# Normed attention and a gated MLP on one Trainium2 core: transfers that wait for their planned time, and a planner with stepwise inputs

## The chip, the core and the metric

The program runs on one core of a Trainium2 chip. The metric is device time in microseconds. Before the change nine runs gave a median of 286.65 us (283.63 to 288.15).

A core has five engines, each with its own instruction queue that it works off strictly in order: TensorE (PE; its weight loads are listed as PEld), VectorE (DVE), ScalarE (ACT), GpSimd (POOL) and SyncE (SP), which here only issues DMA transfers. Engines wait for each other, and for transfers, by semaphores. SBUF is the on-chip memory, PSUM the accumulators that PE writes. A transfer issued by SP or ACT goes through a hardware queue (q1 for SP), one issued by POOL through a software queue (q0).

## What is computed

Eight batches of twelve heads, 448 positions, head size 64. q and k are normed by their root mean square, the scores go through a softmax, and the result, heads side by side (768 columns), goes through a gated MLP with a spatial product.

```python
q_n, k_n = rmsnorm(q, g_q), rmsnorm(k, g_k)        # over the last axis
attn = softmax(q_n @ k_n.T / sqrt(64)) @ v         # per head
x = attn.transpose(0, 2, 1, 3).reshape(8, 448, 768)
h = np.maximum(x @ w_in, 0.0)                      # 768 -> 1024
u, v = h[..., :512], h[..., 512:]
v_n = (v - mean(v)) / sqrt(var(v) + 1e-6)
v_s = einsum('ts,bsd->btd', w_spatial, v_n) + b_spatial[None, :, None]
out = (u * v_s) @ w_out                            # 512 -> 768
```
Inputs and output are float32; the matrix products run in bfloat16.

## The kernel before

**Tiling.** Attention runs over 24 groups G, three per batch, four heads each. For a group, q and k are loaded as 128x896 (`load`, L306), squared (L407 on ACT, L409 on DVE or POOL), summed per row of 64 (`reduce`, L417, always DVE), turned into 1/rms by a logarithm and an exponential on ACT (`rstd`, L423, L424), and scaled to bfloat16 (L431, DVE or POOL). The first six groups are transposed by PE against an identity (`turn`, L448) and copied from PSUM by DVE (`turned`, L457 for q, L459 for k, which also multiplies by the product of g_q and g_k, `g2_col`); the later ones by a DMA transpose (L466). Seven rounds of scores follow (L493, 4 matmuls each, into two PSUM buffers `pss`), each with one exp on ACT over 128x896 (L516). `sums` (L534, 16 matmuls) adds up the exps, `recip` (L541, L542) inverts the sums on ACT, `values` (L552, 2 x 16 matmuls) multiplies by v, and DVE writes the product with the reciprocal into `xt` (L559).

**The MLP** of a batch begins when its six `xt` pieces stand: `unit_v` (L591 for 128 rows, L595 for the last 64), relu on ACT or DVE (L567, L569), row statistics (L615, L616), `ln_rstd` (L622, L623) and `ln_apply` (L630); `unit_u` (L642); `unit_s` (L658), the product with the transposed `w_spatial` (`w_spT`, made by PE, L381); the gate on DVE (L663); `unit_o` (L682, L703), its copy out of PSUM on ACT (L670) or DVE (L672), and the store (L694, L714). Stores go out on SP's queue; in the last batch every second one on ACT's.

**The order** is written by a planner at build time. Every piece of work is a `Task` with a cost (occupancy, latency) on each engine that may do it, a position `pos` in time (smaller is more urgent), tasks that it depends on, PSUM and SBUF buffers that it takes (`get`) or uses, a tile mode on PE (a change of mode costs), and for transfers an earliest time `after` and a length `dma`. The planner goes through simulated time. For each engine it takes the tasks that could start within `LOOK` of the earliest one, and of these the one with the smallest `pos`; the engine whose choice starts first emits its task. Each engine's queue so gets a fixed order. The times of the plan are not in the program: `after` sets a transfer's place in its queue, and a transfer starts when its queue comes to it and its buffer is free.

```python
LOOK = {"PE": 0.15, "ACT": 0.1, "DVE": 0.1, "POOL": 0.2, "SP": 0.2}
...
if t.dma:
    dma = max(dma, at + occ + 1.6) + t.dma
    t.done = dma + 1.3
```
`due(G)` (L291) is the position of a group: 6.3 us apart for the first three, 9.8 for the others. The loads of the first three groups have `after` 0, the others due(G) - 26. There are five raw buffers each for q and k. v of a batch is loaded by four transfers on POOL's queue (L344), w_in by two (L356), w_sp and w_out by one each (L362, L367). [...]

`dummies` (L284) are matmuls on the identity with no use but to keep PE running; `fill` puts them into PE's planned gaps of more than 0.6 us up to 25.5 us. The g rows are loaded by SP (L312, L313), multiplied by DVE (L319), turned into a column by a PE matmul (L326) and copied out of PSUM by DVE (L330).

Of the kernel before, what the change touches and what calls it, by code (L numbers as in the profile page):

```python
# [44 lines left out]
class Task:  # L45
    def __init__(self, name, costs, pos, emit, deps=(), get=(), use=(), mode=None, dma=0.0, after=0.0,
                 port=False):
        self.name, self.costs, self.pos, self.emit = name, costs, pos, emit
        self.deps = [d for d in deps if d is not None]
        self.get = list(get)  # L50
        self.held = list(use)
        self.use = self.get + self.held
        for b in self.use:
            b.left += 1
        self.mode = mode
        self.dma = dma
        self.after = after
        self.port = port
        self.done = None


class Planner:
# [4 lines left out]
    LOOK = {"PE": 0.15, "ACT": 0.1, "DVE": 0.1, "POOL": 0.2, "SP": 0.2}  # L67

    def __init__(self, tc, trace=None):
        self.tc = tc  # L70
        self.tasks = []
        self.trace = trace
        self.port_user = None
# [13 lines left out]
    def add(self, *a, **k):  # L87
        t = Task(*a, **k)
        self.tasks.append(t)
        return t  # L90

    def start_of(self, t, e, free):
        at = max(free[e], t.after)
        if e == "POOL" or (e == "DVE" and t.port):
            at = max(at, self.locked)
        for d in t.deps:
            if d.done is None:
                return None
            at = max(at, d.done)
        if any(b.slot is None for b in t.held):  # L100
            return None
        need = {}
        for b in t.get:
            if b.pool.ordered and b.seq != b.pool.taken + need.get(b.pool, 0):
                return None
            need[b.pool] = need.get(b.pool, 0) + 1
        for p, n in need.items():
            f = sorted(p.free)
            if f[n - 1] == math.inf:
                return None  # L110
            at = max(at, f[n - 1])
        return at

    def run(self, fill=None):
        free = {"PE": 0.0, "ACT": 0.0, "DVE": 0.0, "POOL": 0.0, "SP": 0.0}
        mode, dma = None, 0.0
        self.locked = 0.0
        left = list(self.tasks)
        while left:
            ready = {}  # L120
            for t in left:
                for e in t.costs:
                    at = self.start_of(t, e, free)
                    if at is not None:
                        ready.setdefault(e, []).append((at, t))
            best = None
            for e, c in ready.items():
                end = {}
                first = min(at for at, _ in c)
                for at, t in c:  # L130
                    if at > first + self.LOOK[e]:
                        continue
                    if len(t.costs) > 1:
                        mine = at + t.costs[e][1]
                        other = min(
                            (self.start_of(t, o, free) + t.costs[o][1] for o in t.costs if o != e))
                        if other < mine - 1e-6:
                            continue
                    s = t.pos
                    if e == "PE" and t.mode != mode:  # L140
                        s += 0.6
                    key = (s, at)
                    if best_e_is(end, key):
                        end["k"], end["t"], end["at"] = key, t, at
                if "t" in end and (best is None or end["at"] < best[0]):
                    best = (end["at"], e, end["t"])
            at, e, t = best
            occ, lat = t.costs[e]
            if e == "PE" and t.mode != mode:
                sw = 0.095  # L150
                occ, lat = occ + sw, lat + sw
                mode = t.mode
            if e == "PE" and fill is not None:
                fill(free["PE"], at)
            for b in t.get:
# [3 lines left out]
                p.taken += 1  # L159
            t.emit(e)  # L160
            self.hand_over(t, e)
            free[e] = at + occ
            t.done = at + lat
            if (e == "POOL" and t.dma == 0) or (e == "DVE" and t.port):
                self.locked = at + occ
            if t.dma:
                dma = max(dma, at + occ + 1.6) + t.dma
                t.done = dma + 1.3
# [5 lines left out]
            if self.trace is not None:  # L174
                self.trace.append((at, at + occ, t.done, e, t.name))
            left.remove(t)


def best_e_is(end, key):
    return "k" not in end or key < end["k"]  # L180
# [11 lines left out]
def kernel(  # L192
# [61 lines left out]
    plan = Planner(tc, TRACE)  # L254
# [15 lines left out]
    ident = const.tile([128, 128], BF, name="ident")  # L270
    make_identity(nc, ident)
# [14 lines left out]
    def fill(a, b):  # L286
        if b < 25.5 and b - a > 0.6:
            dummies(int((b - max(a, 2.0) - 0.4) / 0.11))


    def due(G, r=0.0):  # L291
        x = G + r / 7.0
        return 12.0 + (6.3 * x if x < 3 else 18.9 + 9.8 * (x - 3))
# [6 lines left out]
    for G in range(NGT):  # L300
        b, g = divmod(G, NG)
        for i in range(2):
            bf = raw[G, i] = Buf(P_raw[i])

            def emit(e, bf=bf, src=(q_x, k_x)[i][b][g]):
                sync.dma_start(out=bf.t, in_=src)  # L306

            raw_t[G, i] = add(f"load{i} G{G}", {"SP": (0.6, 0)}, due(G) - 26 + i * 0.1, emit, get=[bf], dma=1.4,
                              after=0.0 if G < 3 else due(G) - 26)

    def emit(e):
        sync.dma_start(out=g_row[:, 0], in_=bass.AP(tensor=g_q.tensor, offset=g_q.offset, ap=[[0, 1], [0, 2], [1, D]]))  # L312
# [438 lines left out]
```

## Time and profile before

| | us |
|---|---|
| median of 9 runs | 286.65 |
| lowest, highest | 283.63, 288.15 |
| the profiled execution | 283.63 |
| its span, first to last instruction | 281.9 |
| PE busy | 267.2 |
| ACT busy | 229.0 |
| DVE busy | 195.1 |
| POOL busy | 146.7 |

The mean granted PE clock was 0.997. The 24 loads each of q and k (448 KB) took 5.2 and 6.2 us from issue to landing in the median, the two of w_in (768 KB each) 21.5, w_out 16.1, w_sp 15.6.

In the views below each row gives a start and a length in microseconds, or a busy time. "x16" counts instructions, `out<-in` names tiles without their buffer numbers, and what stands in square brackets is the idle time of the engine before the row and what ended it. In a table of stretches each engine's busy time is followed by its instructions, then come the granted clock (1.00 is full), the share of the DMA engines and GB/s. In a chain of waits each row is the work that released the next.

### The profile page before, as it was taken

Reading aid. Unit: us, or ns where it says so; the run is one execution under the profiler, and the core shown is the slowest. Engines: PE = TensorE matmul, PEld = TensorE weight load, DVE = VectorE, ACT = ScalarE, POOL = GpSimd, SP = SyncE. Lnnn points to the kernel's source line nnn. Section 1 sums busy time; section 2 is a strip of 40 time slices with the busy share of each in tenths; the row PEclk is TensorE's granted clock in tenths of the full one; section 3 lists DMA queues with packets and bytes.
Section 4 is the critical chain, followed back from the end, with each engine's and each line's share of the span. In section 5 each row is a group of like instructions: output and inputs, shape, how many; then the busy total and the mean of one; then the engine's idle time right before and its main releaser. Section 6 shows DMA issues by size and latency. Waiting matters only on the chain.

```text
span 281.9 us, 7090 instructions
## 1 busy us (share of the span) xinstructions
PE 267.2 (95%) x2875; PEld 124.8 (44%) x2875; DVE 195.1 (69%) x332; ACT 229.0 (81%) x369; POOL 146.7 (52%) x122
## 2 busy tenths in 40 slices
PE   7877899999999999999999999999999999999992
PEld 7733464444444444444444444444344443444450
DVE  3986999987777668878885678776775468343630
ACT  4798899978987888878887988879899878676522
POOL 8131546177595776896888497498885000000000
PEclk9999999999999999999999999999999999999998
DMA  7999999477999899995999589998992460007006
GB/s 246 322 294 244 274 282 161 49 195 123 214 221 199 195 177 242 229 242 119 255 240 224 155 205 223 171 305 189 175 216 50 98 165 2 0 12 189 1 5 191
DMA packets 65450, 50.01 MB, mean 177 GB/s; under 512 B 41929, under 2 KB 61898, under 8 KB 65418
## 3 DMA queue, kind: packets, MB, share of 16 engines
q1 hardware_dynamic: 51274, 40.61, 59.6%
q0 software_dynamic: 13824, 8.27, 20.8%
q10 hardware_dynamic: 320, 0.69, 0.7%
q8 instruction: 22, 0.36, 0.5%
q14 instruction: 10, 0.08, 0.1%
HBM read 38.55 MB, written 11.01 MB: 176 GB/s over the span
## 4 chain that ended last, share of the span: by engine, by line
PE 71%; DMA 11%; ACT 6%; DVE 4%; POOL 3%; issue 3%; ACTq 1%; SPq 0%; POOLq 0%; DVEq 0%
PE ps L642 12%; PE pss L493 11%; PE ps L552 11%; PE ps L591 10%; PE ps L658 8%; PE ps L682 8%; PE ps L534 6%; DMA vt<-in_v_dram 5%; ACT et L516 3%; DMA kr<-nk 3%; DMA qf<-in_q_dram 2%; PE ps L595 2%; ACT osb L670 1%; PE ps L703 1%; DVE ms L417 1%
## 5 line engine op out<-in xcount | busy, mean ns | idle before, releaser
L516 ACT ACTIVATE et<-pss 128x896 bf16<-128x896 f32 x168 | 144.0, 916 | 13.4 <-PE pss L493 13.0
L417 DVE TENSOR_REDUCE ms<-sq 128x14 f32<-128x896 f32 x48 | 51.5, 1074 | 8.1 <-ACT sq L407 4.2
L493 PE MATMUL pss<-qT,kT 64*64 64x448 bf16 x672 | 50.3, 362 | 5.7 <-ACT et L516 3.8
L431 POOL TENSOR_TENSOR nq<-qf,rs 128x896 bf16<-128x896 f32 x19 | 32.1, 1688 | 39.5 <-ACT rs L424 32.8
L559 DVE TENSOR_TENSOR xt<-ps,rc 128x448 bf16<-128x448 f32 x48 | 29.4, 623 | 17.6 <-PE ps L552 11.3
L552 PE MATMUL ps<-et,vt 128*32 128x448 bf16 x768 | 41.1, 354 | 0.5 <-DMA vt<-in_v_dram 0.5
L642 PE MATMUL ps<-xt,w_in 128*128 128x448 bf16 x192 | 40.3, 354 | 0.0
L409 POOL TENSOR_TENSOR sq<-kf 128x896 f32<-128x896 f32 x18 | 30.2, 1680 | 14.1 <-DVE nk L431 8.0
L431 POOL TENSOR_TENSOR nk<-kf,rs 128x896 bf16<-128x896 f32 x19 | 32.1, 1688 | 10.1 <-PE ps L448 7.3
L682 PE MATMUL ps<-w_out,gt 128*128 128x384 bf16 x192 | 34.8, 327 | 0.6 <-DVE gt L663 0.6
L591 PE MATMUL ps<-w_in,xt 128*128 128x512 bf16 x144 | 33.7, 380 | 0.0
L663 DVE TENSOR_TENSOR gt<-ps,us 128x448 bf16<-128x448 f32 x32 | 19.9, 623 | 15.6 <-PE ps L658 13.2
L409 POOL TENSOR_TENSOR sq<-qf 128x896 f32<-128x896 f32 x16 | 27.0, 1685 | 6.2 <-DVE kT L474 2.4
L493 PEld LDWEIGHTS <-kT 64*64 64x64 bf16 x672 | 14.3, 104 | 35.9 <-issue 32.3
L658 PE MATMUL ps<-w_spT,vn 128*128 128x448 bf16 (+1 forms) x128 | 27.7, 354 | 0.0
L552 PEld LDWEIGHTS <-vt 128*32 128x32 bf16 x768 | 18.7, 96 | 19.8 <-issue 7.8
L642 PEld LDWEIGHTS <-w_in 128*128 128x128 bf16 x192 | 17.0, 98 | 21.2 <-issue 7.6
L672 DVE COPY osb<-ps 128x384 f32<-128x384 f32 x28 | 15.5, 556 | 14.3 <-PE ps L682 8.9
L615 DVE BATCH_NORM_STATS2 s<-vs 128x6 f32<-128x512 bf16 (+1 forms) x32 | 22.0, 687 | 4.5 <-ACT vs L567 4.1
L682 PEld LDWEIGHTS <-gt 128*128 128x128 bf16 x192 | 17.1, 98 | 17.5 <-issue 6.2
L534 PE MATMUL ps<-et,ones 128*32 128x448 bf16 x384 | 22.8, 355 | 0.1
L344 POOL DMA_DIRECT2D vt<-in_v_dram x32 | 21.6, 692 | 0.0
(65 smaller groups left out, 265.6 us busy)
## 6 DMA issues: line engine op xcount, KB each, us to landing
qf<-in_q_dram SPq DMA_DIRECT2D x24, 448.0 KB, 5.2
kf<-in_k_dram SPq DMA_DIRECT2D x24, 448.0 KB, 6.2
out_dram<-osb SPq DMA_DIRECT2D x45, 192.0 KB, 2.9
vt<-in_v_dram POOLq DMA_DIRECT2D x16, 192.0 KB, 7.5
vt<-in_v_dram POOLq DMA_DIRECT2D x16, 144.0 KB, 8.3
w_in<-in_moe_w_in_dram POOLq DMA_DIRECT2D x2, 768.0 KB, 21.5
out_dram<-osb SPq DMA_DIRECT2D x15, 96.0 KB, 3.7
w_out<-in_moe_w_out_dram POOLq DMA_DIRECT2D x1, 768.0 KB, 16.1
```

What stands on the lines that cost most here:

```text
L409: eng_of[e].tensor_tensor(out=sqb.t, in0=r.t, in1=r.t, op=ALU.mult)
L417: dve.tensor_reduce(out=ms.t[:, i], in_=sqb.t.rearrange("p a (s d) -> p (a s) d", d=D), axis=AX.X, op=ALU.add)
L431: eng_of[e].tensor_tensor(out=nb.t.rearrange("p s a d -> p a s d"), in0=r.t.rearrange("p a (s d) -> p a s d", d=D), in1=P_rs[G % 4][:, i]. ...
L493: pe.matmul(out=ps[64 * h:64 * h + 64, a, 0:S], lhsT=kb[64 * a:64 * a + 64, slot, 64 * xk:64 * xk + 64], rhs=qb[64 * a:64 * a + 64, :, 64 ...
L516: act.activation(out=eb.t[:, r], in_=bf.t[:, :, 0:S], func=AF.Exp, bias=0.0, scale=1.0)
L534: pe.matmul(out=bf.t[32 * l:32 * l + 32, 0:S], lhsT=ones[:, (0 if c < 3 else 1 + x), :], rhs=eb.t[:, r, a, :], start=(c == 0), stop=(c == ...
L552: pe.matmul(out=bf.t[32 * l:32 * l + 32, 0:S], lhsT=vb.t[:, 2 * (g + 3 * a) + x, c, half::2], rhs=eb.t[:, r, a, :], start=(c == 0), stop=( ...
L559: dve.tensor_tensor(out=xb.t[:, j * S:j * S + S], in0=bf.t[:, 0:S], in1=rc.t, op=ALU.mult)
L591: pe.matmul(out=bf.t, lhsT=xb.t[:, j * S + 128 * c:j * S + 128 * c + 128], rhs=w_in[:, j, DH:DF], start=(j == 0), stop=(j == 5))
L642: pe.matmul(out=bf.t[:, 0:S], lhsT=w_in[:, j, 128 * f:128 * f + 128], rhs=xb.t[:, j * S:j * S + S], start=(j == 0), stop=(j == 5))
L658: pe.matmul(out=bf.t[:, 0:S], lhsT=vn.t[0:kp, c, 128 * f:128 * f + 128], rhs=w_spT[0:kp, c, :], start=(c == 0), stop=(c == 3))
L682: pe.matmul(out=bf.t[:, 0:384], lhsT=gt.t[:, f, 128 * c:128 * c + 128], rhs=w_out[:, f, 384 * h:384 * h + 384], start=(f == 0), stop=(f == 3))
```

## The change

1. **Transfers.** A transfer with `after` above 0 gets a semaphore wait (`hold_back`) for the ACT or DVE instruction that ended last in the plan before the transfer's planned start. Its planned length changes (w_in 4.8 to 4.0, w_sp 3.0 to 2.2, w_out 5.0 to 4.5, stores 1.4 to 1.6, the tail of a transfer 1.3 to 0.9), and `after` of several.
2. **Planner.** A dependence can be a pair (task, early): the task may start `early` before the other is done, as its later steps alone need it. `LOOK` is larger, waiting costs `WAIT` per microsecond in the choice, and an engine can have a `bias` against a task.
3. **Parts.** Group 0's squares and reduces are halved (ACT alone squares there), its scaling, transposes and copies are cut in 4 and 3 of 7. `sums` and `values` of groups 0 to 2 are cut in 3 + 1 rounds, `unit_v0` and `unit_v1` of batch 0 in 4 + 2 steps.
4. **Queues.** The g rows are loaded from POOL's queue, ahead of the identity. In the last batch every second store goes on POOL's queue, not ACT's.
5. `fill` takes gaps from 0.4 us.

```diff
+def stepwise(deps, step):
+    return [(d, step * i) for i, d in enumerate(deps)]
...
-    LOOK = {"PE": 0.15, "ACT": 0.1, "DVE": 0.1, "POOL": 0.2, "SP": 0.2}
+    LOOK = {"PE": 0.3, "ACT": 0.9, "DVE": 1.1, "POOL": 0.6, "SP": 0.2}
+    WAIT = 4.0
+    SWITCH = 0.095
+    KEEP = 0.6
...
+    def hold_back(self, t, at, first):
+        ended = [x for x in self.recent if x[0] <= at + 0.2]
+        if t.dma and t.after > 0 and ended:
+            self.tc.add_manual_dep(
+                first, max(ended, key=lambda x: x[0])[1].name,
+                mybir.DependencyInfo(mybir.DependencyClass.Sync, mybir.DependencyReason.DATA),
+                reason="transfer")
...
-                    s = t.pos
+                    s = t.pos + self.WAIT * (at - first)
...
-                t.done = dma + 1.3
+                t.done = dma + 0.9
...
+    for i, g in enumerate((g_q, g_k)):
+        pool.dma_start(out=g_row[:, i], in_=bass.AP(tensor=g.tensor, offset=g.offset, ap=[[0, 1], [0, 2], [1, D]]))
     make_identity(nc, ident)
...
-        if b < 25.5 and b - a > 0.6:
-            dummies(int((b - max(a, 2.0) - 0.4) / 0.11))
+        if b < 25.5 and b - a > 0.4:
+            dummies(int((b - max(a, 2.0) - 0.25) / 0.11))
...
-        return 12.0 + (6.3 * x if x < 3 else 18.9 + 9.8 * (x - 3))
+        return 11.0 + (6.6 * x if x < 3 else 19.8 + 9.6 * (x - 3))
...
-                              after=0.0 if G < 3 else due(G) - 26)
+                               after=0.0 if G < 3 else (9.0, 20.0, 27.0)[G - 3] if G < 6 else due(G) - 26)]
...
-    g_t = add("g2", {"DVE": (0.3, 0.3)}, due(0) - 2.5, emit, deps=[g_t])
+    g_t = add("g2", {"DVE": (0.3, 0.3)}, -90.0, emit, after=6.2)
...
-                                 use=[bf] if parts else [], dma=1.4, after=9.0 if b == 0 else due(3 * b) + (2 if b == 1 else -8)))
+                                 use=[bf] if parts else [], dma=1.4, after=4.0 if b == 0 else 33.0 if b == 1 else due(3 * b) - 8))
...
-        w_t.append(add("w_in", {"POOL": (0.9, 0)}, 5.0, emit, dma=4.8, after=13.0))
+        w_t.append(add("w_in", {"POOL": (0.9, 0)}, 0.0, emit, dma=4.0, after=10.0 + 4.0 * a))
...
-    wsp_load = add("w_sp", {"POOL": (1.0, 0)}, 29.0, emit, dma=3.0, after=18.0)
+    wsp_load = add("w_sp", {"POOL": (1.0, 0)}, 29.0, emit, dma=2.2, after=24.0)
...
-    wout_t = add("w_out", {"POOL": (1.0, 0)}, 36.0, emit, dma=5.0, after=34.0)
+    wout_t = add("w_out", {"POOL": (1.0, 0)}, 36.0, emit, dma=4.5, after=36.0)
...
+        halves = [slice(0, 1), slice(1, 2)] if G == 0 else [slice(0, 2)]
...
+                if G == 0:
+                    costs = {"ACT": costs["ACT"]}
...
+                        bias={"ACT": 0.5 if G == 1 else 5.0} if G else None,
...
+            pieces = [(0, 4), (4, NS)] if G == 0 else [(0, NS)]
...
+        cuts = [(0, 3), (3, 4)] if G < NG else [(0, 4)]
+        need = [[(exps[G, r], 0.19 * max(0, (r % 3 if r < 6 else 3) - c0)) for r in range(6 if c1 < 4 else 7)]
+                for c0, c1 in cuts]
...
+            for j0, j1 in [(0, 4), (4, 6)] if b == 0 and c < 2 else [(0, 6)]:
...
-            a = add(f"unit_s{f} b{b}", {"PE": (0.757, 1.02)}, pos, emit, deps=vns + wspT_t, get=[bf], use=[vn], mode="G")
+            a = add(f"unit_s{f} b{b}", {"PE": (0.757, 1.02)}, pos, emit, deps=stepwise(vns, 0.19) + wspT_t, get=[bf], use=[vn], mode="G")
...
-                    (act if y and b == B - 1 else sync).dma_start(out=o[2 * c + y], in_=ob.t[64 * y:64 * y + 64, :])
-            add(f"store{c} b{b}", {"SP": (0.9 if b < B - 1 else 0.5, 0)}, pos + 1, emit, deps=cs, use=[ob], dma=1.4)
+                    (pool if y and b == B - 1 else sync).dma_start(out=o[2 * c + y], in_=ob.t[64 * y:64 * y + 64, :])
+            add(f"store{c} b{b}", {"SP": (1.2, 0) if b < B - 1 else (0.6, 0)}, pos + 1, emit, deps=cs, use=[ob], dma=1.6)
```

## The prediction

> **What bounds the kernel now.** I read the page first, then the busy time by stretches, the chain of waits of the first 40 us, the timelines of its start and end, and the rows of one tile.
>
> ```profile
> PE 267.2 (95%) x2875; PEld 124.8 (44%) x2875; DVE 195.1 (69%) x332; ACT 229.0 (81%) x369; POOL 146.7 (52%) x122
> DMA  7999999477999899995999589998992460007006
> ```
> TensorE (PE) is the bound on average, and the DMA engines are full for the first 35 us. By stretches (columns: PE, PEld, DVE, ACT, POOL, clock, DMA, GB/s):
>
> ```profile
> 10.00:15.00 5.00, 3.29 (x47) 2.49 (x44) 4.98 (x6) 3.54 (x7) 0.00 (x0) 1.00 1.20 303
> 20.00:25.00 5.00, 4.22 (x70) 2.00 (x67) 2.11 (x4) 4.45 (x9) 0.00 (x0) 1.00 1.06 246
> 50.00:60.00 10.00, 10.00 (x120) 4.53 (x112) 9.91 (x17) 9.12 (x14) 4.66 (x3) 1.00 0.48 76
> 36.45:260.00 223.55, 222.10 (x2414) 96.79 (x2414) 159.45 (x276) 191.49 (x311) 130.65 (x94) 1.00 0.84 172
> ```
> From 36.45 to 260 us PE is idle for 223.55 - 222.10 = 1.45 us in all. Its matmuls are the same in both programs (only 5 dummies fewer), so beyond these 1.45 us a new order can win only by fewer changes of tile mode, in the start and in the tail. The chain of waits of the start:
>
> ```profile
> 4.39 2.04 POOL vt L344 x3
> 6.42 15.48 DMA vt<-in_v_dram
> 22.04 1.71 PE ps L552 x31
> 23.77 0.06 DVE xt L559
> ```
> The first v load lands at 21.90, and PE, whose queue is in order, stops before `values` of group 0. The timeline shows what else was late:
>
> ```profile
> 7.44 0.14 DVE L330 COPY g_col<-ps 128x1 f32<-128x1 f32 x1
> ...
> 13.21 0.57 PE L493 MATMUL pss<-qT,kT 64*64 64x448 bf16 x8 [1.05 <-DVE kT L459]
> ...
> 13.93 7.37 ACT L516 ACTIVATE et<-pss 128x896 bf16<-128x896 f32 x9
> ...
> 23.09 1.31 DVE L559 TENSOR_TENSOR xt<-ps,rc 128x448 bf16<-128x448 f32 x2 [2.83 <-PE ps L552]
> ```
> VectorE (DVE) sat 2.83 us behind the v load. ScalarE (ACT) sets the pace by 21 exps (0.82 us each: nine in 7.37) for groups 0 to 2; the last ended at 35.9.
>
> **The first scores (group 0 in parts, g rows on GpSimd).** GpSimd (POOL) now issues two g loads before it builds the identity. Their issue is not in the trace: by the other POOL issues it lies at 0.58 (w_sp) to 0.82 (w_out), and below that at 0.37 (SP's bias load). I take 0.6, since they are the smallest. The identity, ready at 1.37, comes 1.2 us later (0.7 to 1.6). 38 dummies wait for it and run 0.11 each (43 in 4.77), until 6.8. Behind them stands the g2 matmul; its copy on DVE started 0.87 after it (6.57 to 7.44), so now at 7.7. DVE's new order puts this copy ahead of three of the four half reduces, which therefore all wait for it. A whole reduce costs 1.07 at a pitch of 1.0; a half lies between 0.5 and 0.65, and I take 0.54: the last ends at 9.45, against 7.51 before. Ln and exp follow 0.77 later as before (10.2; before 8.28). During them DVE squares k of group 1 (1.0). Then come four scaled pieces (2.15, from 10.45) and four turned pieces (0.33, 0.26, 0.38, 0.30): kT is complete at 13.9, before 13.16. What the split pipelines, the g2 wait takes. First exp 14.4, before 13.93.
>
> **Squares leave ACT.** ACT squared eleven times at 0.95, now once and in four halves; DVE does three squares more, POOL five. ACT's own time is not the limit there, DVE's queue is. After kT of group 0 DVE holds two reduces, a square, a reduce, two scaled, qT, a reduce and kT before group 1 can be scored: 2.0 + 1.0 + 1.0 + 2.0 + 0.56 + 1.0 + 0.62 = 8.2, so 22.1; before, kT of group 1 ended at 18.28. ACT's order has rstd of group 2 ahead of group 1's exps, and it needs the reduce that ends at 21.5; with rstd (0.6) and the reciprocal (1.15) the first exp of group 1 starts at 23.4 and the seventh ends at 29.2 (before 27.9). Group 2 adds 7 x 0.82, a reciprocal, an rstd (0.58) and some 0.4 of waits: 37.1, against 35.9. **1.2 us later.**
>
> **Transfers wait.** q and k of group 3, w_in, w_sp, the later v and w_out now wait for an ACT or DVE instruction. Only six q/k loads (2.7 MB) and v (0.67 MB) run at first: at the 303 GB/s of the row at 10 to 15 us that is 11 us from 2 us, so v lands near 13 and is not needed before 21. This removes PE's 0.45 and DVE's 2.83; the 1.2 above has that in it. What is queued behind a held load: on SP other loads, transposes and stores, on POOL squares and scalings. The holds name the plan's neighbour in time, and five raw buffers lie between a load and its use, so I take 0, with 0 to +2 as bounds (a late transpose already cost 9.37 us of the chain at 142 us, and PE only 0.2 there).
>
> [...]
>
> ```profile
> L344 POOL DMA_DIRECT2D vt<-in_v_dram x32: 662/687/823, 4.3 to 202.3; - x32
> ...
> DMA to landing us min/median/max: 3.5/7.9/15.5
> ```
> [...] The sum goes by the row, 0.
>
> **PE fills its waits (stepwise inputs).** Two pieces of unit_v (8 matmuls, 1.73) and the sums in parts go ahead of the last exps; in exchange w_sp's transposes (2.0) come later. The comparison is made where batch 0's v units go on. Before, that is 40.87. The new order has by then done 12 score matmuls (0.75) and those 8 more, so level is 40.87 + 0.75 + 1.73 = 43.4. Following ACT on (two exps, reciprocal, two exps from 37.7: the buffers of the third score block come free at 42.2) PE gets there at 42.2 + 0.5 + 2.0 = 44.7, or 43.4 if ACT does not hold it. I take **+1.0** for the start, with bounds -2 (the g2 wait not binding: kT of group 1 then 1.5 earlier, and the waits of 0.5) and +3.
>
> **Steady state.** Mode changes on PE after group 2's scores: 200 become 192. One costs 0.10 to 0.11 (unit_s of 4 matmuls takes 0.76 after a wide unit, 0.86 to 0.87 after values): **-0.85**. Nine relu, five vs and some k scalings pass from ACT to DVE, some 11 us over 200, beside PE. The 1.45 us of idle time I keep; bounds -1.45 and +2.
>
> **Tail.** The second stores go from ACT's queue to POOL's.
>
> ```profile
> 275.55 0.84 PE L703 MATMUL ps<-w_out,gt 128*64 128x384 bf16 x8
> ...
> 277.35 0.49 ACT L670 ACTIVATE osb<-ps 128x384 f32<-128x384 f32 x1 [0.65 <-ACT osb L670]
> ...
> 277.87 0.50 ACTq L714 DMA_DIRECT2D out_dram<-osb  x1
> ```
> PE ended at 276.39, the last copy started at 277.35, because ACT had issued three stores (0.5 each). Now it can start at 276.55: -0.8. POOL's issue is longer by 0.2, and its landing lies between ACT's 3.0 and 3.5 (the shortest v load): **-0.3**, bounds -0.8 and +0.5.
>
> The sum, on the profiled execution (283.63: span 281.9 and 1.7 around it): 283.63 + 1.0 - 0.85 - 0.3 = 283.5. But this was the fastest of nine; the median is 3.0 above it. The trace does not show what the slower ones lose. A v load that lands later moves everything behind it, which the change would end; if it is something else, the 3.0 stay. I take a little under half: **284.8**.
>
> **Rivals.**
> *The spread goes and the start gains* (0.26): with v at 13 nothing of 0.45 and 2.83 is left and the copy of g2 is not late: 283.5 less 2 to 3 from the start, 281 to 283 as a median. For it: v heads the chain. Against: DVE's order.
> *DVE becomes the bound, slower* (0.26): DVE is at 9.91 of 10 in 50 to 60 us already. The new order gives it 2.5 us more work before batch 0's last xt; where a DVE square or scaling meets a POOL one it doubles (2.14 instead of 1.08 at 27.66), three times being 3.2. If PE waits for these, 283.63 + 2.5 + 3.2 = 289.3, and up to 292 with the spread. It decides where kT of group 1 is later than 23.5 or PE is idle over 3 us between 36 and 62.
> *The holds do nothing* (0.08): the named instructions were done long before, v still lands at 20 or later: 286.65 - 0.85 - 0.3 = 285.5.
>
> **How the numbers follow.** My case has 0.40, with its own range from 282.5 to 287.5. About 1% is what a measurement tells from no change: below 283.8 is faster, above 289.5 slower. Faster: the first rival and a quarter of my case, 0.36. Slower: 0.26. Within: 0.38. The range that leaves out 2 in 10 goes from 281 to 291.
>
> **What would show it.** Right: v landed before 16; the g2 copy after 7.3; first exp at 14 to 15; kT of group 1 at 21.5 to 23; PE idle under 2 us from 44 to 260; osb of the last rows within 0.3 of PE's end. Wrong: a first exp before 13; PE waiting for a DMA in mid run; runs spread over 3 us as before.

## The result, and the profile after

The changed kernel takes 287.94 us (median of 17 runs, 287.17 to 289.43; an eighteenth, at 285.98, is on record beside them), the kernel before 286.52 (54 runs, 282.99 to 289.03): a ratio of 1.0091, 95% interval 1.0065 to 1.0116. It is about 0.9% slower; the forecast was 284.8, 0.65% faster. Medians here are over all runs of a kernel; ratios leave disturbed runs out.

| profiled execution | before | after |
|---|---|---|
| time | 283.63 | 287.95 |
| span | 281.9 | 286.2 |
| PE's last matmul ends | 276.39 | 279.19 |
| from there to the span's end | 5.51 | 7.01 |
| mean granted clock | 0.997 | 0.985 |

So 2.80 of the 4.3 us lie ahead of PE's end and 1.50 behind it. The page of the changed kernel has, against the rows shown of before, 15 us more on DVE, 12 us less on ACT and the same PE time. One slice in 40 has a much lower clock (the lower last slice is there before, too):

```profile
PE 267.8 (94%) x2870; PEld 125.2 (44%) x2870; DVE 209.7 (73%) x357; ACT 217.5 (76%) x348; POOL 157.2 (55%) x132
...
PEclk9999995999999999999999999999999999999998
```

The start of the changed kernel in its timeline. The copy of g2 ends at 8.07 and the reduces stand behind it; the first scores go at 13.83, the first exp at 14.57, and the exps of group 1 at 23.25:

```profile
7.91 0.16 DVE L361 COPY g_col<-ps 128x1 f32<-128x1 f32 x1 [0.78 <-PE ps L357]
...
13.83 0.89 PE L550 MATMUL pss<-qT,kT 64*64 64x448 bf16 x8 [0.31 <-DVE kT L512]
...
14.57 2.54 ACT L573 ACTIVATE et<-pss 128x896 bf16<-128x896 f32 x3 [4.32 <-PE pss L550]
...
23.25 6.64 ACT L573 ACTIVATE et<-pss 128x896 bf16<-128x896 f32 x8
```

The busy time by stretches answers the row 36.45 to 260 of before (columns: PE, PEld, DVE, ACT, POOL, clock, DMA, GB/s). After:

```profile
42.10:48.95 6.85, 6.85 (x71) 4.69 (x67) 5.15 (x10) 2.48 (x4) 3.93 (x3) 0.50 1.02 248
60.00:80.00 20.00, 18.84 (x211) 8.76 (x208) 18.55 (x25) 16.73 (x28) 13.19 (x8) 1.00 0.77 186
80.00:260.00 180.00, 179.77 (x1940) 78.10 (x1939) 135.10 (x237) 149.48 (x234) 109.86 (x79) 1.00 0.86 175
```

Before, in the same stretches:

```profile
42.10:48.95 6.85, 6.85 (x54) 3.23 (x54) 6.35 (x12) 6.79 (x12) 4.32 (x5) 1.00 1.03 161
60.00:80.00 20.00, 20.00 (x224) 8.63 (x222) 15.31 (x26) 18.22 (x31) 14.02 (x10) 1.00 0.84 206
80.00:260.00 180.00, 178.55 (x1920) 76.38 (x1913) 121.21 (x212) 151.06 (x244) 105.57 (x76) 1.00 0.83 171
```

Two things are to be seen. After 49 us the two are level in PE's idle time: the new order has 1.16 us between 60 and 80 and 0.23 later, where before had 1.45. And between 42.10 and 48.95 PE is busy all the time, at a granted clock of 0.50. What stands ahead of that stretch, on PE and on DVE:

```profile
39.46 0.94 PE L618 MATMUL ps<-et,vt 128*32 128x448 bf16 x16
41.47 0.60 PE L412 MATMUL ps<-ident,w_sp 64*64 64x64 bf16 x9 [1.07 <-DVE xt L627]
...
43.00 2.28 PE L412 MATMUL ps<-ident,w_sp 64*64 64x64 bf16 x35
45.21 1.04 PE L660 MATMUL ps<-w_in,xt 128*128 128x512 bf16 x2
```

```profile
37.79 0.97 DVE L422 CAST w_spT<-bst 1x448 bf16<-1x448 f32 x1
38.79 1.09 DVE L449 TENSOR_TENSOR sq<-qf 128x896 f32<-128x896 f32 x1
39.80 1.08 DVE L449 TENSOR_TENSOR sq<-kf 128x896 f32<-128x896 f32 x1
40.80 0.62 DVE L627 TENSOR_TENSOR xt<-ps,rc 128x448 bf16<-128x448 f32 x1
```

PE has written the values of group 2 and needs a PSUM buffer that only DVE's `xt` can free; two of the four are held by the begun pieces of `unit_v`. DVE has a row copy of the bias and two squares ahead of that `xt`, so PE stands still for 1.07 us. Then come 35 narrow transposes of w_sp in a row. The end of the chain of waits is now on POOL:

```profile
279.24 0.52 POOL out_dram L765
279.76 0.23 issue
279.99 0.55 POOLq L818
```

Its last row, at 279.99, is at the time of POOL's last store; the span ends at 286.2, 5.6 us after that row's end. What fills these 5.6 us stands among the instructions of the program's last line (L818, before L746). Each row gives the shortest, the median and the longest of its instructions in ns, then the first and the last start. After, and then before:

```profile
L818 POOLq DRAIN  x3: 46/99/5400, 280.0 to 285.9; - x3
L818 SPq DRAIN  x3: 7/7/7, 283.9 to 285.7; - x3
...
L746 POOLq DRAIN  x3: 46/93/6298, 214.2 to 281.6; - x3
L746 SPq DRAIN  x3: 7/7/13, 281.0 to 281.3; - x3
```

Each engine has two or three such DRAINs; SyncE's first stands behind its waits for the last stores (3.1 us after, 2.1 before). After the change SyncE is at that point at 283.9, but POOL's long DRAIN stands behind its last store and lasts from 279.99 to 285.39; the span ends 0.78 us later. Before, POOL's long DRAIN began at 214.2, at its last scalings, and was over by 220.5; there the span ends 0.8 us after SyncE's DRAIN.

### The profile page after: what moved, and what is told of

Its sections match the earlier page's. It is cut to its first block, busy times and chain, and to the rows that moved or that the text cites. A ratio compares the mean times of both kernels' runs of the same rounds, so it can differ in the third digit from the quotient of the medians.

```text
span 286.2 us, 7162 instructions
## 1 busy us (share of the span) xinstructions
PE 267.8 (94%) x2870; PEld 125.2 (44%) x2870; DVE 209.7 (73%) x357; ACT 217.5 (76%) x348; POOL 157.2 (55%) x132
## 4 chain that ended last, share of the span: by engine, by line
PE 66%; issue 19%; DVE 7%; ACT 3%; POOL 2%; POOLq 0%; DVEq 0%
PE pss L550 11%; PE ps L618 10%; PE ps L713 10%; PE ps L660 8%; PE ps L753 7%; PE ps L729 7%; PE ps L597 5%; ACT et L573 2%; PE ps L664 2%; DVE ms L462 1%; DVE sq L449 1%; PE ps L320 1%; DVE nq L483 1%; PE ps L774 1%; POOL nk L483 1%
## 5 line engine op out<-in xcount | busy, mean ns | idle before, releaser
L462 DVE TENSOR_REDUCE ms<-sq 128x14 f32<-128x896 f32 (+1 forms) x50 | 51.3, 1038 | 5.6 <-ACT sq L447 3.5
L550 PE MATMUL pss<-qT,kT 64*64 64x448 bf16 x672 | 51.7, 365 | 3.9 <-ACT et L573 2.5
L483 POOL TENSOR_TENSOR nq<-qf,rs 128x896 bf16<-128x896 f32 x17 | 28.7, 1689 | 39.8 <-ACT rs L470 29.6
L449 POOL TENSOR_TENSOR sq<-qf 128x896 f32<-128x896 f32 x20 | 33.7, 1686 | 12.3 <-DVE nk L483 4.1
L483 POOL TENSOR_TENSOR nk<-kf,rs 128x896 bf16<-128x896 f32 x20 | 33.8, 1689 | 5.7 <-DVE nq L483 3.4
L449 POOL TENSOR_TENSOR sq<-kf 128x896 f32<-128x896 f32 x19 | 31.9, 1681 | 9.0 <-DVE sq L449 4.0
L660 PE MATMUL ps<-w_in,xt 128*128 128x512 bf16 x144 | 35.5, 386 | 0.1
L550 PEld LDWEIGHTS <-kT 64*64 64x64 bf16 x672 | 15.0, 104 | 34.9 <-issue 30.1
L618 PEld LDWEIGHTS <-vt 128*32 128x32 bf16 x768 | 19.4, 97 | 18.0 <-issue 5.1
L765 POOL DMA_DIRECT2D out_dram<-osb x3 | 1.7, 557 | 44.9 <-ACT osb L741 44.9
L597 PE MATMUL ps<-et,ones 128*32 128x448 bf16 x384 | 23.4, 355 | 0.3 <-ACT et L573 0.3
```

What stands on the lines that cost most here:

```text
L449: eng_of[e].tensor_tensor(out=sqb.t[:, h], in0=r.t[:, h], in1=r.t[:, h], op=ALU.mult)
L462: dve.tensor_reduce(out=ms.t[:, i, h], in_=sqb.t[:, h].rearrange("p a (s d) -> p a s d", d=D), axis=AX.X, op=ALU.add)
L483: eng_of[e].tensor_tensor(out=nb.t.rearrange("p s a d -> p a s d")[:, :, s0:s1, :], in0=r.t.rearrange("p a (s d) -> p a s d", d=D)[:, :, s ...
L550: pe.matmul(out=ps[64 * h:64 * h + 64, a, 0:S], lhsT=kb[64 * a:64 * a + 64, slot, 64 * xk:64 * xk + 64], rhs=qb[64 * a:64 * a + 64, :, 64 ...
L597: pe.matmul(out=bf.t[32 * l:32 * l + 32, 0:S], lhsT=ones[:, (0 if c < 3 else 1 + x), :], rhs=eb.t[:, r, a, :], start=(c == 0), stop=(c == ...
L618: pe.matmul(out=bf.t[32 * l:32 * l + 32, 0:S], lhsT=vb.t[:, 2 * (g + 3 * a) + x, c, half::2], rhs=eb.t[:, r, a, :], start=(c == 0), stop=( ...
```

## The experiments

Seventeen kernels besides the two, and the changed one again (e12). All are named e1 to e18; "ratio" is to the kernel before on the same chip.

### The tail: e1, e8

e1, in the changed kernel:

```diff
-  (pool if y and b == B - 1 else sync).dma_start(out=o[2 * c + y], ...)
+  (act if y and b == B - 1 else sync).dma_start(out=o[2 * c + y], ...)
```

> The changed kernel with the second stores of the last batch back on ScalarE's queue. After the last store was issued 6.2 us passed to the end of the span in the changed kernel, 4.0 before. Theory (a store issued by GpSimd lands later): the last issue comes 0.5 later than with GpSimd's queue at most, the end after it at 4.0, 1.3 to 2.0 us less: about 286.3. Rival (the end waits for something else, the stores on SyncE's queue for instance): within 0.5 of 287.9.

Measured 286.34 (285.94 to 287.26, 10 runs), ratio 1.0067 (1.0036 to 1.0098). This is 1.6 under the changed kernel as a median, but by the ratios (1.0091 there) only 0.7, since the kernel before was faster beside e1 (284.93). The profile is plainer: PE ends at 278.60 and the span at 284.2, 5.60 instead of 7.01 later, and POOL's long DRAIN lies at 229.3 to 235.8. e8 makes the opposite edit in the kernel before:

```diff
-  (act if y and b == B - 1 else sync).dma_start(out=o[2 * c + y], ...)
+  (pool if y and b == B - 1 else sync).dma_start(out=o[2 * c + y], ...)
```

> The kernel before with the second stores of the last batch on POOL's queue instead of ACT's, nothing else. Theory (a store on POOL's queue ends about 2 us later than on a hardware queue, and the copies that it frees on ACT do not bring that back): span end 6.0 to 6.5 us after the last store's issue, where before has 4.0, and the median 1.0 to 2.0 us over that of before. Rival (the 2 us of e1 are something that only the new plan's end has): within 0.5 us of before.

Ratio 1.0063 (0.9990 to 1.0135): not told from nothing by its time alone. Its profile is clear. PE ends at 281.60 and the span at 288.2, 6.60 after it, where before has 5.51; the last store is issued at 282.42, so the span ends 5.8 after it, a little under what was expected (6.0 to 6.5). POOL's long DRAIN has moved to the end here as well:

```profile
L746 POOLq DRAIN  x3: 46/99/4986, 282.4 to 287.9; - x3
```

It is not the landing: the four POOL stores of the changed kernel landed 3.5 to 3.6 us after their issue, ACT's in before 3.0 to 3.2. The last one so landed near 283.6, and the span went on for 2.6 us, up to the end of POOL's DRAIN and 0.78 more. All twenty profiles are of one of two kinds. In the six where POOL issues the last stores (the changed kernel twice, e2, e3, e4, e8), the DRAIN ends 4.4 to 4.9 us after POOL's last row, and the span 0.8 after the DRAIN. In the other fourteen the DRAIN was over 48 to 61 us before the end (3.0 to 3.3 us after POOL's last scaling), and the span ends 0.8 after SyncE's DRAIN. In the changed kernel SyncE's DRAIN alone would have let the span end 1.45 earlier. What fills POOL's DRAIN, the trace does not show.

### The holds: e2, e7

e2 is the changed kernel without the waits of `hold_back`, in the same order:

```diff
-        if t.dma and t.after > 0 and ended:
+        if False and t.dma and t.after > 0 and ended:
```

> The changed kernel without the semaphore waits of its transfers; order and everything else as they are. Theory A (the holds give v and the first groups the DMA engines alone, but later nothing depends on them): v lands after 16 instead of 11 to 13, still before 21 or a little later, 287 to 289, and the runs spread by 3 us again. Theory B (held loads on SyncE's queue make transposes and squares late): 1 to 3 us less. Theory C (the holds do nothing): the same trace, 287.9 within 0.4.

289.62 (288.83 to 290.31, 4 runs), 1.7 slower than with them as a median (ratio 1.0175 (1.0111 to 1.0240), beside 1.0091). From the chain of waits of its first 45 us:

```profile
8.06 14.54 DMA vt<-in_v_dram
22.74 0.75 PE ps L618 x11
```

v takes 14.54 us to land instead of 5.2 to 5.7, PE waits 1.2 for it, and group 1's first exp goes from 23.25 to 24.77. Given to the kernel before alone (same order, waits added):

```diff
+            self.hold_back(t, at, done[n])
+            if e in ("ACT", "DVE"):
+                self.recent = self.recent[-7:] + [(at + occ, done[-1])]
```

> The kernel before with the hold_back waits alone; the order on every engine is that of before. Theory (the waits keep later loads out of the way of those that are needed first, and are worth something with any plan): the wait for v at the values goes from 0.5 to 0, and the median is 0.5 to 1.5 us under that of before at the same clock. Rival (they only mend what the new plan's earlier loads make late): within 0.5 us of before. Worse by over 0.5: the waits delay something that was in time.

Ratio 1.0060 (1.0011 to 1.0109): slower. The wait for v is gone, as expected, but in the profile PE loses 5.1 us between 180 and 240, where before's loses 0.7. A DMA transpose of k stands in the chain of waits there:

```profile
203.18 9.07 DMA kr<-nk
```

That the added waits made it late is not shown: e10 below, without them, loses 2.5 between 150 and 210. What the two runs say together is that the holds belong to a plan: they pay where `after` was set with them, and cost something here.

### The start: e3

```diff
-        pool.dma_start(out=g_row[:, i], ...)
+        act.dma_start(out=g_row[:, i], ...)
```

> The changed kernel with the two g rows loaded from ScalarE's queue, so that GpSimd builds the identity first, at 1.4 instead of 3.1. Theory (the copy of g2 holds three reduces): copy at about 6.4 instead of 7.9, first exp at 13.0 to 13.4 instead of 14.6, and all up to the first xt 1.2 to 1.5 earlier: 286.4 to 286.8. Rival (from group 1 on VectorE's and ScalarE's queues give the gain back, or the PE clock takes it): first exp earlier, time within 0.5 of 287.9.

288.26 (287.24 to 289.13, 4 runs): no gain. The identity is ready 1.7 us earlier, the g2 copy only 0.33 (7.58), and in the profiled run k of group 1 landed late (7.54 us), so that the first exp came at 15.17.

### The half clock: e4, e9, e11, e13, e16, e17, e18

A scan of the granted clock in stretches of 0.5 us shows it at 0.50 in pieces of 3.41 to 3.42 us or a multiple (6.83 mostly, 13.65 once, in e8), and at 1.00 otherwise, in every profile. Beyond the last microseconds the profile of before has none, the changed kernel one of 6.83 at 42. e4 puts ten 64-column dummies behind the values of group 2, into the gap:

```diff
+                    for _ in range(10 if last else 0):
+                        pe.matmul(out=bf.t[:, 448:512], lhsT=ident, rhs=ident[:, 0:64], ...)
```

> The changed kernel with ten more dummy matmuls (64 columns each, into unused columns of the accumulator) right after the values of group 2, where PE is idle from 40.4 to 41.5 waiting for xt. Theory (PE's granted clock fell to 0.50 from 42.1 to 48.9 because PE had idled): the clock stays above 0.99 and 2.0 to 3.4 us go: 284.5 to 286. Rival 1 (the clock falls for another reason, such as the narrow transposes of w_sp): clock 0.985 again, 287.9 or up to 0.5 more. Rival 2 (in these 7 us PE had slack): clock 0.99 and more, time within 0.5 of 287.9.

287.67 (287.48 to 288.90, 4 runs): not cured; PE's wait was 0.66 instead of 1.07, and a piece of 3.42 us lay at 45.9 to 49.4. e9 leaves the 49 narrow transposes out:

```diff
-                    pe.matmul(out=ps[64 * y:64 * y + 64, t, 0:64], lhsT=x, rhs=ident[0:64, 0:64],
-                              is_transpose=True, ...)
+            for n in range(m // 64):
+                pe.matmul(out=bf.t[:, 0:S], lhsT=ident, rhs=w_in[:, c, 0:S], ...)
```

> The changed kernel with the last stores of e1; the 49 narrow 64x64 transposes of w_sp are left out and seven 448-column matmuls of the full array stand in their place (so w_spT holds something else), 14 narrow ones by two wide ones; the order is that of e1 otherwise. Theory (narrow transposes count as little activity and bring, or keep, the half clock of 42 to 49): no half clock between 41 and 50, mean clock 0.993 or more, and 283.5 to 285.0, of which some 0.8 is the shorter work (35 x 0.065 = 2.3 against 5 x 0.3 = 1.5). Rival (the idle 1.07 us at 40.4 alone does it): the spell stays, one or two pieces of 3.42 us between 41 and 50, and 285.3 to 286.3.

284.97 (284.48 to 286.07, 10 runs), and no half clock between 41 and 50, with PE's wait of 1.06 still there. I read this as "the transposes do it". But the block had also become 0.9 us shorter (35 in 2.28 against five in 1.37), so the time proves less than the clock. e11 keeps the transposes and adds a wide matmul ahead of each group of them:

```diff
+            pe.matmul(out=bf.t[:, 0:S], lhsT=ident, rhs=w_in[:, c, 0:S], start=True, stop=True)
```

> The changed kernel with the last stores of e1 and one 448-column matmul of the full array ahead of each of the four groups of w_sp transposes, into the same PSUM buffer, which the transposes then overwrite (4 x 0.19 to 0.36 us more of PE). Theory (low activity between 40 and 45 brings the half clock, and a little wide work lifts it): at most one piece of 3.42 us, 285.0 to 286.0. Rival (as e1, and the added work is paid): 286.3 plus 0.8 to 1.4, 287 to 288.

287.69 (287.48 to 288.38, 4 runs), one piece of 3.42 at 46: the added work was paid and little won. e13 does the same transposition with 28 pieces of 128x64 instead of 49 of 64x64:

```diff
-    w_sp = const.tile([64, NS, S], BF, name="w_sp")
+    w_sp = const.tile([128, 4, S], BF, name="w_sp")
...
+                    pe.matmul(out=ps[64 * y:64 * y + 64, 128 * t:128 * t + n], lhsT=x, rhs=ident[0:n, 0:n],
```

> The changed kernel with the last stores of e1, and w_sp loaded with two of its rows t beside each other on 128 partitions (two loads on POOL's queue instead of one), so that 28 transposes of 128x64 do what 49 of 64x64 did; the same order otherwise, the same result. Theory (the narrow transposes hold PE's activity down and keep the half clock): one piece of 3.42 us or none between 41 and 50, and PE 21 x 0.065 = 1.4 us less work there: 283.5 to 285.0 where e1 has 286.3. Rival (the idle 1.07 us alone brings the spell): pieces of 3.42 us as in e1 or the changed kernel, 284.8 to 286.0.

286.44 (285.32 to 288.38, 10 runs), no better than e1, and a piece at 45.7. The 1.4 us of work were not there to be had: 20 paired transposes took 2.10 us, 35 narrow ones 2.28. What remained was the gap itself. e16 takes e13 and moves most of the bias copy on DVE behind the last w_spT copy:

```diff
+            if c == 3:
+                dve.tensor_copy(out=w_spT[64:65, 3, 64:]..., in_=bst[64:65, :]...)
...
-        dve.tensor_copy(out=w_spT[64:65, 3, :]..., in_=bst[64:65, :]...)
+        dve.tensor_copy(out=w_spT[64:65, 3, 0:64], in_=bst[64:65, :]...[:, 0])
```

> e13 with most of the row copy w_spT<-bst (0.97 us on DVE, ahead of the two squares that PE's wait at 40.4 stands behind) moved behind the last w_spT copy. Theory (that wait is on the path): the wait of 1.07 us shrinks to 0.1 to 0.3, v2 of the gate starts 0.8 to 1.0 earlier, 0.5 to 1.0 us under e13. Rival (DVE is the bound between 36 and 47, so the copy only costs later): within 0.3 us of e13.

285.63 (285.25 to 287.53, 10 runs), 0.8 under e13 as a median (the intervals of their ratios overlap: 0.9987 to 1.0065, and 1.0015 to 1.0083 for e13). The wait shrank from 1.05 to 0.33 and no half clock fell between 41 and 50. (A new wait of 1.3 for `vs` came up behind it, where the moved copy now stands.) e17 and e18 join this to the stores of e15 below and differ in the shape of the transposes alone:

> The changed kernel with paired w_sp transposes (e13), the bias copy behind the last w_spT copy (e16) and all last stores on SP's queue (e15). If the gains add up (e13 286.4, less 1.0, less 0.8): 284.4 to 285.0, 0.2 to 0.8 us under the kernel before on the same chip, range under 3 us. Rival (the two gains overlap, since a later end of PE hides nothing but the clock's luck was in both): 285.2 to 285.7, level with before.

> As e17 with the 49 narrow transposes of the changed kernel. Theory (narrow work holds the clock down): half clock between 41 and 50 in the profile and 0.8 to 2.0 us over e17. Rival (PE's wait ahead of them was the cause, and the shape is worth only its 0.2 to 0.3 us of time): no half clock there, within 0.5 us of e17.

285.10 and 285.07 (12 runs each, 284.63 to 286.57 and 284.64 to 286.53): the shape is worth nothing here. PE in e18, with 35 narrow transposes in a row at full clock:

```profile
40.78 0.60 PE L412 MATMUL ps<-ident,w_sp 64*64 64x64 bf16 x9 [0.33 <-DVE xt L629]
...
42.30 2.26 PE L412 MATMUL ps<-ident,w_sp 64*64 64x64 bf16 x35 [0.19 <-DVE xt L629]
```

Where the changed order stood with its gap (0.66 us in e4, 1.05 to 1.08 in the others) and its transposes, eight profiles of nine (the kernel itself twice, e1 to e4, e11, e13) had the half clock between 41 and 50; the ninth (e15) did not. Of six without the gap (e6, e16, e17, e18) or without the block of transposes there (e5, e9) none had it. The clocks of all runs agree: of 66 runs with both (those behind the nine profiles) two had a mean clock of 0.995 or more, of 44 without one of them (e9, e16 to e18) sixteen. So in these runs it took both, with some chance in it (e15, whose PE rows are those of e13 up to there, kept the full clock), and the gap is the part that can be mended. (e5 and e6 follow.)

### Changing the plan's inputs: e5, e6

```diff
-        a = add(f"w_spT{c}", {"PE": (0.7, 1.0)}, 34.0, ...)
+        a = add(f"w_spT{c}", {"PE": (0.7, 1.0)}, 50.0, ...)
```

> The changed kernel with the last stores of e1 (second stores of the last batch on ACT's queue) and the 28 + 7 narrow 64x64 w_sp transposes planned at 50 instead of 34, so that they no longer stand in a block of 35 behind the 1.07 us in which PE is idle at 40.4. Theory (that block and the idle time before it bring the half clock of 42.1 to 48.95): the rows between 40 and 50 show the full clock, mean clock 0.993 or more, median 284.5 or less. Rival 1 (the clock falls whatever stands there): mean clock 0.987 and 286.3 within 0.5, as e1. Rival 2 (the spell moves with the transposes to where they now stand): a half-clock spell within 3 us of the moved block, 285.5 to 287.

```diff
-            for j0, j1 in [(0, 4), (4, 6)] if b == 0 and c < 2 else [(0, 6)]:
+            for j0, j1 in [(0, 6)]:
```

> The changed kernel with the last stores of e1 and unit_v of batch 0 in one piece, as before the change, so that two begun sums no longer hold two of the four PSUM buffers while DVE squares. Theory (the split makes the wait of 1.07 us for a PSUM buffer, and the wait lets the clock fall): no PE wait for xt over 0.5 us between 39 and 45, mean clock 0.993 or more, 284.0 to 285.0. Rival (the wait only goes elsewhere: unit_v cannot start until the last xt): PE idle between 36 and 46 within 0.5 us of the changed kernel's, clock 0.987, 286.3 within 0.5.

289.39 and 293.29, ratios 1.0108 (1.0015 to 1.0202) and 1.0223 (1.0125 to 1.0321), against 1.0067 for e1. As times they isolate nothing: the planner decided all that follows anew, and PE waited elsewhere (1.3 for `us` in e5, 4.5 for a kT on ACT at 73 in e6). Their clocks tell more. e5 keeps the gap of 1.05 us with 14 transposes behind it and has full clock from 17 to 58; e6 loses the gap, has 35 transposes from 41.29 to 44, and full clock there too, but a half clock at 36.0 to 39.5 and one of 6.82 at the end of its 4.5 us. In e5 the other 35 transposes run into the next gap, 1.32 us at 57.9, and there the clock falls (0.60 in the last row is 0.50 from 58.2 on):

```profile
55.00:56.00 1.00, 1.00 (x28) 0.99 (x22) 1.00 (x4) 0.97 (x3) 0.53 (x1) 1.00 1.06 145
56.00:57.00 1.00, 0.92 (x20) 0.68 (x19) 1.00 (x3) 0.97 (x2) 0.67 (x1) 1.00 1.12 375
57.00:58.00 1.00, 0.85 (x11) 0.83 (x8) 1.00 (x2) 1.00 (x2) 0.00 (x0) 1.00 1.07 392
58.00:59.00 1.00, 0.00 (x0) 0.00 (x0) 1.00 (x2) 0.56 (x1) 0.28 (x1) 0.60 1.30 269
```

PE counts as busy for 2.8 of the 3 us ahead of it, mostly with transposes. The half clock went with the block, as the second rival had said; the time, 289.39, is not that rival's.

### The kernel before: e10, e14

e10 adds dummies to its start (36 instead of 28 ahead of the first transposes, 20 instead of 11 behind them, and so on):

```diff
-        if b < 25.5 and b - a > 0.6:
-            dummies(int((b - max(a, 2.0) - 0.4) / 0.11))
+        if b < 25.5 and b - a > 0.4:
+            dummies(int((b - max(a, 2.0) - 0.25) / (0.11 if a < 6.0 else 0.09 if a < 9.0 else 0.07)))
```

> The kernel before with more dummy matmuls in PE's planned gaps of the first 25.5 us (gaps of 0.4 instead of 0.6 us count, 0.25 instead of 0.4 is left free, and a dummy is taken as 0.09 and then 0.07 us instead of 0.11); all other order is the same. Theory (the kernel before loses its time by luck of where the clock's 3.42-us windows fall on PE's gaps at 8 to 16; its dummies are too few once the clock is up): fast runs at clock 0.99 or more nearly always, median 283 to 284, spread under 2 us. Rival (the spread of before is something else, or dummies delay the first rounds): median within 0.7 of before or worse, same spread.

288.38 (284.42 to 289.84, 10 runs), ratio 1.0055 (0.9997 to 1.0113). The clock came out at 0.983 to 0.999, the time did not: even at 0.998 a run took 286.8. Its profile loses 2.5 us of PE between 150 and 210, behind late scaling on POOL, where before's loses 0.9. e14 gives before the paired transposes of e13:

> The kernel before with the same pairs for w_sp, nothing else changed. In the profile of before the transposes stand at 34.5 to 40.9 between scores that wait for ACT, PE is busy 8.8 of 10 us there: between 0 and 1.4 us less than before, 0.7 taken. Its spread stays (range over 4 us), since its gaps at 8 to 16 and the late POOL work at 150 to 215 are not touched; if the spread goes, the transposes were its cause.

Ratio 0.9995 (0.9953 to 1.0036), the spread as wide as before: no gain, and not the spread's cause.

### The stores on one queue, and the kernel again: e15, e12

e15 is e13 with all stores of the last batch on SP's queue:

```diff
-  (act if y and b == B - 1 else sync).dma_start(out=o[2 * c + y], ...)
+  sync.dma_start(out=o[2 * c + y], ...)
```

> e13 with all stores of the last batch on SP's queue, so that neither ACT nor POOL issues one. ACT's three issues of 0.5 us and the 0.65 us waits behind them leave the path of the copies: last copy within 0.6 us of PE's end (1.4 in e1), last issue some 0.9 earlier less 0.5 for the second issue on the same queue; 0.2 to 0.8 us under e13. Rival: SP's issues queue up behind each other and the end is the same within 0.2.

285.45 (284.38 to 287.46, 10 runs) beside e13's 286.44. From PE's end to the span's end it has 5.07 (e13 5.57). The copies come sooner, as the theory has it (the last starts 0.04 after PE's end instead of 0.97), the last issue does not (1.59 instead of 1.49); the other half microsecond of the median is not placed.

The two profiles give the price of a half clock. Their PE rows differ by no more than 0.01 us from 12 to 45.7, where e13 gets a piece of 3.42 us (45.70 to 49.12) and e15 none. e13, then e15, at the ends of this stretch:

```profile
45.05 0.60 PE L662 MATMUL ps<-w_in,xt 128*128 128x512 bf16 x2
50.58 1.30 PE L715 MATMUL ps<-xt,w_in 128*128 128x448 bf16 x6
...
45.06 0.60 PE L662 MATMUL ps<-w_in,xt 128*128 128x512 bf16 x2
49.07 1.30 PE L715 MATMUL ps<-xt,w_in 128*128 128x448 bf16 x6
```

The piece costs 1.51 us, and these stay up to PE's end (279.04 against 277.53). The changed kernel's rows of the same work go from 45.21 to 50.74: 5.53 us, where e15 takes 4.01.

> The changed kernel unchanged, beside e9 and e11 on the same chip. If the last stores' queue is worth what e1 showed, it stands 1.2 to 2.0 us over a kernel that differs in that alone: 287.5 to 288.2 where the kernel before has 285 to 286.5, at a clock of 0.985.

287.95 (two runs), with the half clock at 43 to 50 and 7.04 from PE's end to the span's, so the changed kernel is the same on another chip.

## Why the prediction was wrong, step by step

The forecast of 283.5 for an execution like the profiled one became 287.95. By its own terms:

| term | forecast | measured |
|---|---|---|
| start, at batch 0's v units | +1.0 (44.7 against a level of 43.4) | +2.1 (45.21 against 43.1) |
| half clock behind that point | not in the sum | +1.5 (5.53 for 4.01, as e15 shows) |
| idle time later | kept | -0.1 (1.68 against 1.75) |
| mode changes | -0.85 | taken as forecast, not measured by itself |
| not placed | | +0.15 |
| up to PE's end | +0.15 | +2.80 |
| tail | -0.3 | +1.50 |

The level is 43.1 and not 43.4 because the new order has done 8 score matmuls more at that point, not the 12 that the prediction counts.

**The step that failed first is the tail.** It said "POOL's issue is longer by 0.2, and its landing lies between ACT's 3.0 and 3.5 (the shortest v load): **-0.3**, bounds -0.8 and +0.5". The copies did what was forecast: the last one starts 0.04 after PE's end. The landing was 3.6, also near. But the span did not end with the landing of the last POOL store (near 283.6 in the changed kernel); it ended behind POOL's long DRAIN, 5.2 to 5.6 us after the end of POOL's last row (e8, changed kernel). e1, e8 and e15 show that the queue is the cause: from PE's end to the span's end it makes 1.4 us against ACT's queue in this plan (e1), 1.1 in the plan of before (e8), and 1.9 against SP's (e15).

**The second is a term that the sum lacked, the clock.** The text took 1.00 for granted everywhere, though it put PE at "44.7" behind a wait for buffers and 2.0 us of transposes. The one run of the changed kernel with a clock of 0.996 took 285.98, 1.97 under the profiled one at 0.985. One run proves little (others took 287.17 at 0.991 and 289.43 at 0.990), but e13 against e15 gives 1.51 for one piece in rows that are otherwise the same. e16 and e18 against e13 and the changed kernel show that it comes with the gap ahead of the transposes, e5 and e9 that the gap without the transposes does not bring it. In e14 the pieces begin at 17.26, 37.73 and 160.61, 20.47 and 122.88 us apart, which is 6 and 36 times 3.41; and in the changed kernel the longest wait of PE from 14 us to the fall at 42.10 was the 1.07 us. Why the clock falls is not shown: in e5 it fell behind 3 us of which PE counts as busy for 2.8, mostly with transposes, while e18's 35 transposes, 2.26 us, ran at full clock.

**The start was right in its mechanism** up to group 1. First exp 14.57 (14.4 forecast), g2's copy at 7.91 (7.7), kT of group 1 at 22.2 (22.1), first exp of group 1 at 23.25 (23.4), v landed by 14 (13). What was short is the stretch from 37: DVE's bias copy and squares ahead of `xt`, 1.07 us on PE. That is the place that the rival "DVE becomes the bound" named; its condition did not come true (PE idle for 26.00 - 24.55 = 1.45 us from 36 to 62, not over 3), nor did its price. All that the prediction listed as signs of being right came true (PE idle for 1.39 us from 44 to 260, the last copy 0.04 after PE's end), and the kernel was slower all the same: none of the signs looked at the clock, or past the last copy.

**The holds** cost nothing (0 forecast, 0 to +2): they gain 1.7 in this plan, by the medians (e2). **GpSimd's issues of transfers**, for which the sum took 0 by the row of v, were as long beside a busier DVE (209.7 us against 195.1): v's 32 took 655 to 804 ns after, 662 to 823 before, where four in a row at 28.81 took 2.69 us with DVE busy all through.

**The spread** was the part that moved the forecast from 283.5 to 284.8, by "a v load that lands later". The change did bring v early, and the runs of the changed kernel do lie closer (287.17 to 289.43, with the one at 285.98 outside). But over the 85 runs of the kernel before, on five occasions, that the ratios of the experiments rest on, time falls by 1.4 us for 0.01 more of mean clock (r = -0.78): 23 runs at 0.995 or more have a median of 283.16, 17 below 0.982 one of 286.43. So most of what the slower runs lose goes with the clock. e10 shows that the clock alone does not bring it back; what else the kernel before loses between 150 and 215 is not settled. This is also why the medians differ by only 1.4 where the profiled executions differ by 4.3: the execution that was profiled was one of the fastest, at a clock of 0.997.

With the three repairs together (stores on SP, bias copy later, either shape) the new plan takes 285.1. This is 1.0% under the changed kernel by the medians (0.8% by the ratios) and level with before: ratios 1.0008 (0.9972 to 1.0045) and 1.0026 (0.9992 to 1.0060). No version here is shown to beat the kernel before; before's best runs (282.7) are under all of them.

## What to carry to other kernels

Sum PE's time with the granted clock as a factor: look for short gaps that lie beside a block of transposes (here, at 0.66 to 1.08 us, eight profiles of nine had the half clock), and price the stretch behind them at half clock if PE is the bound there (1.51 us for a piece of 3.42). Let the engine that closes slowest finish first: POOL's DRAIN ended 3.0 to 4.9 us after its last work in every profile, so a store at the very end belongs on another queue. Look at the closing instructions, too: a chain of waits that ends 5.6 us before the span does not explain the end. And a greedy planner answers one changed number with another program, so isolate an effect by changing what a task emits, in the same order, rather than the plan's inputs.

## What the runs showed of the hardware

- The granted clock was 1.00 or 0.50, in pieces of 3.41 to 3.42 us or multiples; the same program had a mean of 0.969 to 0.996 (changed kernel) or 0.959 to 0.999 (before) from run to run.
- A half clock cost 1.51 us for 3.42 where PE was always busy (e13 against e15), and nothing that shows in the start: e9's profiled run had its piece at 13.55 to 16.96 and took 284.63, its four runs at 0.995 or more 284.78 to 286.07. At half clock the narrow transposes were not slower either (35 in 2.28 us in the changed kernel, in 2.26 at full clock in e18).
- Transposes of 64x64 took 65 ns each (35 in 2.28 us, changed kernel), those of 128x64 105 ns (20 in 2.10, e13); by these numbers 28 in place of 49 are worth some 0.25 us, not 1.4.
- From PE's end to the span's end: 5.0 to 5.1 us with all last stores on SP, 5.4 to 5.7 with ACT's help, 6.5 to 7.0 with POOL's.
- POOL's closing DRAIN ended 3.0 to 3.3 us after its last scaling (fourteen profiles) and 4.4 to 4.9 after its last store (six); the span ended 0.8 us after it or after SyncE's, whichever was later.
